# An adaLN block with sliding-window attention and a token-mixing MLP: normalization work moved between VectorE and GpSimd, the first MLP matmul split by token groups, another written order

## The chip, the cores and the metric

The kernel runs on one core of a Trainium2 chip. A core has five engines with a queue each: TensorE (PE) multiplies matrices from SBUF into PSUM, ScalarE (ACT) evaluates functions, VectorE (DVE) and GpSimd (POOL) do elementwise work, and SyncE (SP) issues DMA transfers. Each engine takes its instructions in order and waits on semaphores where an instruction needs another engine's result. [...]

The metric is the device time of one execution in microseconds. The time before is the median of three runs. A profile of one further execution gives the time of every instruction.

## The reference

One sequence of 2048 tokens with 512 features, in bf16. A condition vector `c` gives six modulation vectors; a windowed attention of 32 heads of 16 features and an MLP over the token axis follow.

```python
mod = (silu(c) @ w_mod).reshape(1, 6, 1, -1)
sa, ca, ga, sb, cb, gb = mod[:, 0], ..., mod[:, 5]
h = layernorm(x) * (1 + ca) + sa
x = x + ga * attention(h, wqkv, wo)      # 32 heads, key j for query i if 0 <= i - j < 256
h = layernorm(x) * (1 + cb) + sb
x = x + gb * B(h)
# B: h = layernorm(h); u = gelu(einsum('bsd,sf->bdf', h, w1) + b1)
#    y = einsum('bdf,fs->bds', u, w2) + b2; transposed back     w1: 2048 x 1792
```

So three layer norms are computed for each token: one ahead of the attention, one behind it with its modulation, and one inside the MLP. The MLP's first matmul sums over all 2048 tokens and gives 1792 rows of 512 features; the second sums over the 1792.

## The kernel before

**Token groups.** The tokens are worked on in four groups G of 512, each of four tiles of 128 tokens (16 tiles `x0` to `x15` in SBUF). For each group, `proj` normalizes and modulates the input, transposes it, and computes queries, keys and values; `attention` does the windowed attention; `post` does the output projection, the second layer norm with its modulation, and the MLP's layer norm. The result of a tile is `hb`, the MLP's input.

**Attention.** It goes by 75 chunks of 512 score columns for four heads at once (15 in group 0, 20 in each other). For chunk i, TensorE computes the scores (S) into four PSUM banks (`pss`, three, and `psb`, one), ScalarE takes the exponential in two instructions (EA of 128x1536 and EB of 128x512) into a bf16 tile `et`, and VectorE multiplies the columns at the window's edges by a 0/1 mask (M, 512 or 1024 columns in all). `et` has seven buffers. Two units of 256 queries share five chunks; when a unit's last mask is done, TensorE multiplies its tiles with the values and with ones (AV, into `po`), ScalarE takes logarithm and exponential of the sums (`lz`), and VectorE multiplies (OT). Keys are stored in two copies with alternate features set to zero (`KT`, split by GpSimd from `kb`), and values in block form (`VT`, placed by GpSimd from `vb` and `vs`).

**Shared banks.** Four banks are the scores' (five with `psb`'s two buffers). Three others, `od0` to `od2`, are shared by everything else that TensorE computes while attention runs: projections, AV, output projection, partial sums of the MLP. Such a bank is free again when its eviction, mostly on VectorE, is done.

**Layer norms.** `norm_ops` gives VectorE one statistics instruction per tile. For the groups of four tiles (`quiet`), GpSimd then combines the statistics in eight instructions on 4 or 8 columns: mean, variance, the power -0.5 (`rs`) and the product of mean and `rs` (`nm`). The first tiles and the last group use ScalarE instead. In `post`, groups 0 to 2 are normalized on GpSimd (`n2`, tile `xn2`, shown as `xn` in the profile), then modulated (`m2`: a product with `bc_cb1` and a sum with `bc_sb`, on VectorE but for two tiles on GpSimd), then normalized again on GpSimd (`hb`).

**The MLP's first matmul.** While attention still runs, `partials` computes for each of the 14 blocks fc of 128 rows the sum over the first 1024 tokens (eight matmuls `p`, evicted as `part`), from chunk 52 on. Its weights come in pieces of 512 KB (1024 tokens x 256 rows). The rest of the sum, over the last 1024 tokens, is `mlp1` (`u`): it starts when the last chunk's attention is under way, adds `part` on VectorE (`ga`), takes the GELU on ScalarE, and multiplies with `bc_gb`. The last part of the kernel is the second matmul (`py`), 16 tiles of 14 matmuls each, added to the input and stored.

**The opening.** SyncE issues the loads of the first two token tiles, two of the four parts of `w_mod`, then `wqkv` in pieces; ScalarE's queue issues the condition vector and the two other parts. TensorE runs filler matmuls (`warm`, eight pairs) on a zero tile; eight of them come first, the rest between and behind the transposes and the modulation matmuls (`fm`). The first key matmul stands behind all of them.

**What sets the order.** All this is a list of operations with names, engines and dependencies. A written list `ORDER` gives the sequence in which they are emitted, and so the order on every engine's queue; a table `CHOSEN` gives the engine where an operation may run on several. A function walks the list and emits. The constants for costs and ready times in the code (`X_READY` and others) take no part in the emitted program when the order is written out: they decide only which of the three shared banks an operation takes.

Almost every instruction of the profile has line 234, that of the wrapper that emits it, so groups are told apart by their tiles.

Of the kernel before, what the change touches and what calls it, by code (L numbers as in the profile page):

```python
# [13 lines left out]
P = 128  # L14
# [12 lines left out]
PART_A = 3  # L27
PART_AT = 20.0
# [3 lines left out]
X_READY = [3.0, 3.75, 11.7, 12.0]  # L32
MOD_READY = [4.7, 6.7, 6.9, 7.4]
W_READY = [8.35, 9.25, 9.25, 11.0, 14.0]
# [26 lines left out]
    2, 38, 3, 9, 40, 1, 10, 11, 4, 12, 41, 13, 14, 42, 16, 39, 8, 43, 44, 45, 17, 46, 18, 48, 47, 19, 6, 20, 7, 51,  # L61
    50, 49, 5, 52, 0, 53, 54, 56, 55, 57, 70, 58, 71, 126, 72, 75, 127, 73, 59, 76, 80, 60, 123, 81, 74, 128, 130,
    77, 61, 78, 82, 85, 131, 79, 86, 84, 83, 89, 63, 62, 132, 134, 87, 64, 124, 135, 65, 15, 67, 68, 66, 90, 88, 69,
    136, 138, 139, 264, 93, 121, 94, 129, 106, 91, 95, 142, 140, 96, 107, 265, 143, 98, 97, 92, 108, 266, 144, 166,
    111, 167, 267, 109, 99, 145, 268, 168, 100, 170, 112, 171, 110, 146, 133, 147, 113, 151, 137, 148, 174, 172,
    115, 152, 149, 173, 102, 175, 103, 150, 114, 141, 27, 104, 153, 269, 184, 176, 28, 494, 154, 156, 185, 271, 270,
    155, 157, 29, 116, 273, 177, 117, 272, 158, 188, 186, 118, 161, 159, 275, 120, 189, 495, 24, 119, 276, 187, 160,
    190, 198, 496, 101, 25, 199, 274, 724, 21, 22, 169, 162, 105, 200, 26, 202, 163, 23, 30, 203, 31, 497, 178, 191,
    498, 164, 206, 204, 179, 165, 32, 207, 180, 192, 193, 277, 194, 278, 181, 216, 208, 182, 279, 217, 183, 280,
    499, 36, 286, 281, 287, 218, 220, 282, 283, 195, 288, 221, 284, 209, 289, 292, 285, 222, 501, 725, 332, 196,  # L70
    293, 333, 290, 205, 298, 201, 299, 503, 294, 334, 336, 197, 295, 210, 291, 337, 37, 211, 34, 33, 212, 505, 125,
    500, 223, 314, 213, 340, 35, 338, 315, 300, 341, 956, 957, 219, 302, 310, 316, 311, 214, 335, 350, 296, 342,
    224, 312, 225, 351, 726, 226, 313, 301, 233, 215, 339, 352, 354, 504, 234, 727, 355, 297, 304, 235, 305, 728,
    356, 343, 364, 230, 227, 306, 365, 231, 357, 307, 317, 318, 232, 228, 368, 958, 366, 353, 344, 229, 369, 345,
    242, 122, 239, 319, 370, 308, 372, 236, 373, 371, 502, 237, 303, 243, 240, 374, 238, 506, 309, 382, 346, 383,
    241, 321, 320, 244, 322, 358, 384, 245, 386, 359, 347, 387, 323, 959, 246, 360, 375, 328, 348, 396, 388, 329,
    349, 508, 397, 324, 325, 330, 507, 361, 400, 729, 398, 367, 401, 516, 326, 247, 517, 399, 376, 518, 362, 404,
    402, 377, 389, 520, 519, 405, 513, 385, 363, 514, 731, 960, 248, 378, 406, 414, 249, 522, 515, 379, 415, 523,
    255, 327, 390, 391, 524, 380, 331, 732, 418, 416, 392, 381, 250, 419, 526, 509, 525, 510, 403, 521, 393, 407,
    428, 730, 420, 528, 511, 733, 429, 529, 408, 251, 734, 530, 430, 432, 417, 512, 540, 394, 256, 433, 531, 409,  # L80
# [32 lines left out]
]  # L113
CHOSEN = {
    "ACT": [
        48, 50, 72, 74, 95, 1017, 1034, 1039,
    ],
    "DVE": [
        47, 49, 51, 52, 66, 69, 77, 79, 82, 84, 87, 91, 97, 100, 104, 108, 110, 113, 115, 118, 120, 248, 250, 252, 254,
        277, 278, 281, 285, 288, 294, 300, 306, 312, 316, 319, 323, 326, 330, 478, 480, 482, 484, 507, 508, 511, 515,  # L120
        518, 524, 530, 536, 542, 546, 549, 553, 556, 560, 708, 710, 737, 738, 741, 745, 748, 754, 760, 764, 767, 771,
        774, 780, 786, 790, 968, 973, 979, 984, 990, 995, 1001, 1006, 1012, 1023, 1028,
    ],
    "POOL": [
        712, 714,
    ],
}
BATCH = True
# [1225 lines left out]
```

## Time and profile before

| | us |
|---|---|
| median of three runs | 257.79 (255.44 to 257.80) |
| profiled execution | 258.61 |
| its span, first to last instruction | 256.8 |
| first exponential starts | 12.89 |
| scores of the last chunk start | 172.40 |
| TensorE busy | 241.1 |
| VectorE busy | 200.6 |
| ScalarE busy | 179.9 |
| GpSimd busy | 133.0 |

The granted TensorE clock is 0.993 of full speed on average.

Lines of a timeline are: start, duration, engine, line, operation, output and inputs by the program's names, count. Lines with shapes ("128x512") give partitions and elements. Busy time of TensorE counts a matmul from start to modelled end, and matmuls overlap; a stretch in which it is 100% busy is not always one at its peak. Instructions on one engine can overlap at their ends too: a VectorE eviction of 0.68 us is followed by the next one 0.60 us after its start.

### The profile page before, as it was taken

The numbers are of one execution on the slowest core, as the hardware profiler recorded it, in microseconds if no ns is written. First come the engines' busy times: TensorE is split into PE (matmuls) and PEld (weight loads), VectorE is DVE, ScalarE is ACT, GpSimd is POOL, SyncE is SP. The second block draws the span as 40 slices with busy tenths as digits, with TensorE's granted clock in tenths as the row PEclk, the third lists the DMA queues.
The fourth block names the chain that finished last, engine by engine and source line by source line (L and its number), as shares of the span: only waits on it lengthen the run. The fifth ranks groups of instructions, "written<-read, shape, count | busy, mean of one in ns | idle before, by whom it ended". The sixth has DMA issues, their size and how long they took to land.

```text
span 256.8 us, 8133 instructions
## 1 busy us (share of the span) xinstructions
PE 241.1 (94%) x3427; PEld 122.2 (48%) x3427; DVE 200.6 (78%) x392; ACT 179.9 (70%) x255; POOL 133.0 (52%) x237
## 2 busy tenths in 40 slices
PE   7988989899998999979999999999999999999994
PEld 2665635444443454434545454446444444444443
DVE  4589999998899999998658879799869864444442
ACT  4399999999999999998999999998138510000000
POOL 8288977999999897896914389190000000000000
PEclk9999999999999999989999999999999999999999
DMA  7998360246254400060030003351899601111111
GB/s 222 326 349 252 12 80 3 42 114 159 61 120 60 116 3 3 9 182 0 5 92 14 3 3 84 106 142 37 326 332 387 232 22 41 58 48 41 41 43 41
DMA packets 41341, 27.02 MB, mean 105 GB/s; under 512 B 11992, under 2 KB 37208, under 8 KB 41304
## 3 DMA queue, kind: packets, MB, share of 16 engines
q1 hardware_dynamic: 41008, 25.97, 36.2%
q8 instruction: 27, 0.44, 0.7%
q10 hardware_dynamic: 296, 0.53, 0.6%
q14 instruction: 10, 0.08, 0.1%
HBM read 22.03 MB, written 2.10 MB: 94 GB/s over the span
## 4 chain that ended last, share of the span: by engine, by line
PE 61%; POOL 12%; DVE 10%; ACT 8%; issue 4%; DMA 3%; SPq 0%; DVEq 0%; POOLq 0%
PE pu L234 20%; PE py L234 19%; PE po L234 7%; ACT et L234 6%; PE pss L234 6%; POOL VT L234 4%; PE pa L234 3%; DVE et L234 3%; POOL xn L234 3%; POOL KT L234 2%; PE pk L234 2%; DMA w1p<-in_B_w_dram 2%; PE pv L234 2%; ACT lz L234 1%; DVE vb L234 1%
## 5 line engine op out<-in xcount | busy, mean ns | idle before, releaser
L234 ACT ACTIVATE et<-pss 128x1536 bf16<-128x1536 f32 x75 | 110.8, 1477 | 3.3 <-PE psb L234 1.7
L234 PE MATMUL pu<-hb,w1p 128*128 128x512 bf16 x224 | 52.6, 380 | 0.0
L234 DVE TENSOR_TENSOR et<-et,maskt 128x1024 bf16<-128x1024 bf16 (+2 forms) x79 | 48.5, 628 | 2.7 <-ACT et L234 2.6
L234 PE MATMUL py<-guT,w2r 128*128 128x512 bf16 (+1 forms) x238 | 48.7, 366 | 0.5 <-DVE otile L234 0.5
L234 ACT ACTIVATE et<-psb 128x512 bf16<-128x512 f32 x75 | 46.9, 626 | 0.0
L234 PE MATMUL pss<-QT,KT 32*128 32x64 bf16 (+3 forms) x720 | 30.0, 232 | 6.6 <-ACT et L234 5.0
L234 PEld LDWEIGHTS <-w2r 128*128 128x128 bf16 x238 | 23.3, 98 | 26.0 <-issue 0.7
L234 PE MATMUL po<-et,VT 128*32 128x64 bf16 (+3 forms) x960 | 32.3, 237 | 1.0 <-DVE kb L234 0.6
L234 PEld LDWEIGHTS <-w1p 128*128 128x128 bf16 x224 | 20.4, 98 | 25.0 <-issue 2.5
L234 PE MATMUL po<-et,ones_bd 128*32 128x256 bf16 (+3 forms) x624 | 32.0, 271 | 0.0
L234 POOL TENSOR_SCALAR KT<-kb,mask_par 128x512 bf16<-128x512 bf16 (+1 forms) x38 | 27.4, 732 | 7.2 <-ACT kb L234 5.8
L234 DVE TENSOR_TENSOR otile<-py,xr 128x512 bf16<-128x512 f32 (+1 forms) x17 | 11.2, 660 | 25.3 <-PE py L234 25.2
L234 PEld LDWEIGHTS <-KT 32*128 32x128 bf16 x960 | 15.8, 93 | 31.1 <-issue 28.9
L234 PE MATMUL psb<-QT,KT 32*128 32x64 bf16 (+3 forms) x240 | 29.5, 232 | 0.0
L234 PEld LDWEIGHTS <-VT 128*32 128x32 bf16 x960 | 19.6, 97 | 12.9 <-issue 10.7
L234 POOL TENSOR_SCALAR xn<-x,rs,nm 128x512 bf16<-128x512 bf16 x24 | 22.8, 951 | 1.4 <-DVE h L234 0.5
L234 DVE BATCH_NORM_STATS2 st<-x 128x6 f32<-128x512 bf16 x32 | 21.4, 682 | 2.2 <-DMA x<-in_A_x_dram 2.1
L234 PE MATMUL pk<-h1T,wqkv 128*128 128x256 bf16 (+2 forms) x108 | 21.3, 326 | 0.6 <-DVE vb L234 0.5
L234 PEld LDWEIGHTS <-wqkv 128*128 128x128 bf16 x164 | 13.8, 99 | 13.4 <-issue 6.0
L234 DVE TENSOR_TENSOR OT<-po,lz 128x256 bf16<-128x256 f32 x32 | 13.3, 416 | 8.2 <-ACT lz L234 8.2
L234 PE MATMUL pv<-wqkv,h1T 128*64 128x256 bf16 (+1 forms) x112 | 17.2, 321 | 0.4 <-DVE OT L234 0.4
L234 PE MATMUL pa<-wod,OT 128*128 128x512 bf16 x64 | 17.0, 380 | 0.4 <-DVE kb L234 0.2
(99 smaller groups left out, 324.1 us busy)
## 6 DMA issues: line engine op xcount, KB each, us to landing
w1p<-in_B_w_dram SPq DMA_DIRECT2D x14, 512.0 KB, 5.0
w2r<-in_B_w_dram SPq DMA_DIRECT2D x14, 512.0 KB, 7.8
x<-in_A_x_dram SPq DMA_DIRECT2D x16, 128.0 KB, 5.2
wmod<-in_w_mod_dram SPq DMA_DIRECT2D x4, 512.0 KB, 8.6
out_dram<-otile SPq DMA_DIRECT2D x15, 128.0 KB, 1.7
wqkv<-in_A_wqkv_dram SPq DMA_DIRECT2D x4, 256.0 KB, 4.9
vs<-vb SPq DMA_DIRECT2D x24, 32.0 KB, 3.0
wmod<-in_w_mod_dram ACTq DMA_DIRECT2D x2, 256.0 KB, 3.7
```

What stands on the lines that cost most here:

```text
L234: ins = call(*args, **kwargs)
```

## The change

1. **Second layer norm and modulation.** The normalization `n2` goes. Two scalar-tensor-tensor instructions on VectorE compute (x - mean) * `bc_cb1` and then that * `rs` + `bc_sb`, for all 16 tiles.
2. **Statistics.** Five of the small instructions that combine the statistics go to VectorE (a tensor-tensor and four scalar-tensor-tensor ones); GpSimd keeps the power and, for two of the three norms, the product `nm`.
3. **Masks.** M may run on VectorE or GpSimd; 21 of the 75 run on GpSimd by the new table (chunks 1, 7, 25, 31, 41 to 46, 50, 51, 59, 62 to 64, 66 to 69, 73), and two instructions of the third group's input modulation.
4. **First MLP matmul.** For blocks 0 to 9, the first 1024 tokens become two groups of 512: the first (`pE` below, four matmuls, evicted as `part`) needs only group 0's `hb`, the second is added to it on VectorE (`pd`). Blocks 10 to 13 stay whole. Weights come in quarters of 256 KB.
5. **Opening.** The second token tile is loaded by ScalarE's queue, ahead of the condition vector; the parts of `w_mod` change queues. The fillers are eight, then two, one and two matmuls at fixed places; two stand between the last `fm` and the first key matmul.
6. **Order.** `ORDER` and `CHOSEN` are written anew.

In the new order, the first groups of blocks 0 to 9 stand between the scores of chunks 42 and 56, and the second groups follow from chunk 58; the last group's projections reach to chunk 60 (58 before). Around one place, TensorE's two lists are:

```
before: ... S45 q3.1 AV40 S46 S47 AV41 AV42 k3.2 S48 AV42 AV43 AV44 S49 v3.2 k3.3 S50 ...
after:  ... S45 pE1 k3.0 S46 q3.0 AV40 q3.0 S47 AV41 AV42 v3.0 S48 v3.1 AV42 AV43 S49 ...
```

GpSimd's and VectorE's new lists around the masks of chunks 41 to 46 (l2pw is the power; "ke", "qe", "ve", "peE" are evictions):

```
GpSimd:  M42 l2pw M41 M43 M44 M45 M46 vo M50 kk M51 ...
VectorE: OT M40 peE2 m2 peE1 ke m2 OT qe m2 ve M47 ve OT m2 peE4 M48 M49 peE5 ...
```

The core of the diff:

```diff
     load_x(0)
-    load_x(1)
-    load_mod(0, nc.scalar)
-    load_mod(1, dma)
-    load_mod(2, nc.scalar)
-    load_mod(3, dma)
+    load_mod(0, dma)
+    load_mod(1, nc.scalar)
+    load_mod(2, dma)
+    load_mod(3, nc.scalar)
...
+    load_x(1, nc.scalar)
+    nc.scalar.dma_start(out=c4[:], in_=c.rearrange("o (j p) -> (o j) p", p=P))
...
+    warms = warm_ops(4, 2, [])
...
+    warms += warm_ops(2, 1, [o5])
...
+        fms[0].deps.append(transposed[0][0])
+        warms.extend(warm_ops(1, 1, fms[0:1]))
+        fms[1].deps.append(warms[-1])
+        warms.extend(warm_ops(2, 1, fms[-1:]))
...
-            po.tensor_tensor(out=mv[:], in0=st[:, :, 1:3], in1=st[:, :, 4:6], op=ALU.add)
-            po.tensor_tensor(out=mv[:], in0=mv[:], in1=halves[:, 0:n, :], op=ALU.mult)
-            po.tensor_tensor(out=sq[:], in0=st[:, :, 1], in1=st[:, :, 4], op=ALU.subtract)
-            po.tensor_tensor(out=sq[:], in0=sq[:], in1=sq[:], op=ALU.mult)
-            po.tensor_scalar(out=sq[:], in0=sq[:], scalar1=0.25, scalar2=EPS, op0=ALU.mult, op1=ALU.add)
-            po.tensor_tensor(out=sq[:], in0=sq[:], in1=mv[:, :, 1], op=ALU.add)
-            po.tensor_tensor(out=rs[:], in0=sq[:], in1=power[:, 0:n], op=ALU.pow)
-            po.tensor_tensor(out=nm[:], in0=mv[:, :, 0], in1=rs[:], op=ALU.mult)
+            var = mv[:, :, 1]
+            ve.tensor_tensor(out=sq[:], in0=st[:, :, 1], in1=st[:, :, 4], op=ALU.subtract)
+            ve.scalar_tensor_tensor(out=var, in0=st[:, :, 2], scalar=D * EPS, in1=st[:, :, 5], op0=ALU.add, op1=ALU.add)
+            ve.scalar_tensor_tensor(out=mv[:, :, 0], in0=sq[:], scalar=-0.5, in1=st[:, :, 4], op0=ALU.mult, op1=ALU.subtract)
+            ve.scalar_tensor_tensor(out=sq[:], in0=sq[:], scalar=0.25, in1=sq[:], op0=ALU.mult, op1=ALU.mult)
+            ve.scalar_tensor_tensor(out=var, in0=var, scalar=1.0 / D, in1=sq[:], op0=ALU.mult, op1=ALU.add)
+
+        def e_pw(e):
+            _, mv, rs, nm = box[key]
+            po.tensor_tensor(out=rs[:], in0=mv[:, :, 1], in1=power[:, 0:n], op=ALU.pow)
+            if tag != "l2":
+                po.tensor_tensor(out=nm[:], in0=mv[:, :, 0], in1=rs[:], op=ALU.mult)
...
-            def e_n(e, tl=tl, j=j):
-                xn2[tl] = late.tile([P, D], BF, name="xn2", tag="xn2")
-                normalize(e, xn2[tl][:], xres[4 * G + tl][:], ("l2", G, own[0]), j)
-
-            def e_m(e, tl=tl):
+            def e_m(e, tl=tl, j=j):
+                _, mv, rs, _ = box["l2", G, own[0]]
                 u = h2[tl] = late.tile([P, D], BF, name="h2", tag="h2", bufs=4)
-                ENGINE[e].tensor_tensor(out=u[:], in0=xn2[tl][:], in1=bc_cb1[:], op=ALU.mult)
-                ENGINE[e].tensor_tensor(out=u[:], in0=u[:], in1=bc_sb[:], op=ALU.add)
+                ve.scalar_tensor_tensor(
+                    out=u[:], in0=xres[4 * G + tl][:], scalar=mv[:, j, 0:1], in1=bc_cb1[:],
+                    op0=ALU.add if shifted else ALU.subtract, op1=ALU.mult,
+                )
+                ve.scalar_tensor_tensor(
+                    out=u[:], in0=u[:], scalar=rs[:, j : j + 1], in1=bc_sb[:], op0=ALU.mult, op1=ALU.add,
+                )
...
+        def group(fc, lo, deps, pos, first):
+            hi = 8 if first and fc >= EARLY or not first else 4
...
+            def e_pe(e):
+                if first:
+                    part[fc] = box["A" if fc < EARLY else "B"].tile([P, D], F32, name=f"part{fc}")
+                    copy(e, part[fc][:], box["p", fc][:])
+                else:
+                    ve.tensor_tensor(out=part[fc][:], in0=box["p", fc][:], in1=part[fc][:], op=ALU.add)
...
+        for fc in range(EARLY):
+            pos = start_of(2) + EARLY_AT + fc * EARLY_STEP
+            early[fc] = group(fc, 0, [loads[fc // 2, 0], *done[:4]], pos, True)
...
+            if fc < EARLY:
+                g = group(fc, 4, [loads[fc // 2, 1], *done[4:]], pos, False)
+            else:
+                g = group(fc, 0, [loads[fc // 2, 0], loads[fc // 2, 1], *done], pos, True)
...
-                    ve.tensor_tensor(out=dst, in0=dst, in1=msk, op=ALU.mult)
+                    ENGINE[e].tensor_tensor(out=dst, in0=dst, in1=msk, op=ALU.mult)
```

`normalize` is unchanged. In the new order the load of the last exchanged value tile (`vs`) stands on SyncE's queue behind ten loads of `w1` quarters.

## The prediction

> **What bounds the kernel now.** I read the busy shares first, then busy time by stages, then the timeline of each boundary. Over the whole span TensorE looks like the only limit:
>
> ```profile
> PE 241.1 (94%) x3427; PEld 122.2 (48%) x3427; DVE 200.6 (78%) x392; ACT 179.9 (70%) x255; POOL 133.0 (52%) x237
> ```
>
> The stages say otherwise (columns: stretch, its length, then busy us of PE, PEld, DVE, ACT, POOL; clock, DMA share, GB/s):
>
> ```profile
> 12.90:20.00 7.10, 5.94 (x95) 4.32 (x94) 6.37 (x16) 6.58 (x11) 6.05 (x11) 1.00 1.10 348
> 20.00:50.00 30.00, 26.94 (x570) 15.56 (x568) 29.10 (x62) 29.98 (x42) 25.56 (x45) 1.00 0.38 70
> 50.00:98.00 48.00, 44.67 (x850) 21.93 (x851) 45.93 (x89) 47.41 (x65) 44.55 (x76) 1.00 0.40 87
> 98.00:120.00 22.00, 19.29 (x375) 9.69 (x373) 20.55 (x38) 20.64 (x27) 17.35 (x32) 0.92 0.21 57
> 120.00:172.40 52.40, 52.22 (x915) 25.62 (x914) 41.71 (x74) 51.72 (x72) 31.29 (x49) 1.00 0.21 55
> ```
>
> From the first exponential (12.89) to the scores of the last chunk (172.40) ScalarE is busy 156.3 of 159.5 us: it waits 0.52 + 0.02 + 0.59 + 1.36 + 0.68 = 3.2 us in all. That stage is ScalarE's: 75 chunks at 1.477 + 0.626 us of exponentials, plus logarithms and reciprocals. From 172.40 to 251.6 TensorE never stops; its chain is fixed work (last attention outputs, the rest of the partial sums, 56 pairs of the second half, 238 output matmuls), and the end is at 256.8: **84.4 us of tail**. So the time is: first exponential + ScalarE's work + ScalarE's waits + tail. VectorE (95 to 97% from 20 to 98) and GpSimd (93%) count only where they make ScalarE or that tail wait.
>
> **Opening.** The first exponential is late by a queue, not by data:
>
> ```profile
> 7.98 2.72 PE L234 MATMUL pss<-warm 128*128 128x512 bf16 x6
> 8.50 0.86 DVE L234 TENSOR_SCALAR h1T<-h1T,modFM 128x256 bf16<-128x256 bf16 x3
> 10.49 0.49 PE L234 MATMUL pss<-h1T,wqkv 128*128 128x128 bf16 x4
> ```
>
> The operands are ready at 9.36, but six filler matmuls stand in front of the first key matmul. After the change two stand there, one more between the first two modulation matmuls, and 16 fillers become 13. Without the queue the key matmul comes 10.49 - 9.36 = 1.1 us earlier. The weights' landing (4.7 to 5.5 us after an issue at 2.7) isn't later, as SyncE issues three loads ahead of them, not four. Against it: all four modulation matmul groups now follow the second transpose, two of which ran before it. I take -1.0, bounds -1.3 (the second input tile, landing at 4.42 behind the first, comes by its own queue: 0.28 us of VectorE's wait) and 0.
>
> **ScalarE's work.** From the two written orders: behind the first exponential it loses two 128x256 evictions (0.38 each) and gains two such and one of 128x512 (0.59 long, 0.48 start to start, as for the partial sums): +0.5. The exponentials, logarithms and reciprocals are the same. This has no cover: the stage is ScalarE's.
>
> **VectorE and GpSimd, by durations.** VectorE loses 21 masks: 13 of 128x1024 (0.750), 7 of 128x512 (0.506), one of the first group (0.79): 14.1; 14 products and 14 sums of the modulation (0.435 + 0.580): 14.2; four normalizations (0.61): 2.4; two modulations of the transposed input (0.428): 0.9. It gains 32 scalar-tensor-tensor instructions; the nearest row is the one with an f32 output, 0.743: 23.8 (from below the tensor-tensor rows, 0.435 to 0.580: 13.9 to 18.6). Then nine groups of five instructions on 4 columns (0.15 to 0.18 each): 7.2; ten additions into partial sums (0.688): 6.9. Sum +6.3 us. GpSimd loses seven of eight small instructions per statistics group (six in the two kinds that keep the product): a group takes 3.7 to 3.9 now and 1.1 to 1.4 after, nine times 2.5: 22; twelve normalizations (0.951): 11.4; two modulations (1.310 + 1.594): 5.8. It gains the masks: not in the trace there; nearest are its tensor-tensor rows, 1.310 for 512 columns, so 2.6 for 1024: 13 x 2.6 + 7 x 1.3 + 2.0 = 45 (from below, by 0.76, its shortest 512-column form with one input, 26), and the two modulations, 0.9 each. Sum +8. Neither is on the path by its sum: VectorE's additions fall mostly behind 98, where it idles 1.5 + 10.7 us, and GpSimd's masks too (17 of the 21 belong to chunks 41 and later), where it idles 4.7 + 21.1. What hides them is ScalarE's stage; if VectorE falls behind, its evictions hold the three PSUM banks that projections, attention outputs and partial sums share, and scores queued behind them on TensorE make ScalarE wait.
>
> **First MLP matmul split.** The number of matmuls is the same. Ten half groups move ahead, between chunks 42 and 56; projections of the last group and the output projection of group 2 move behind them, so that TensorE's work ahead of chunk 55 is equal within 1 us, and behind the last scores the same pairs are left in both orders, less one attention output of 0.2 us. The tail therefore stays: **-0.2**. The split does fill one hole:
>
> ```profile
> 110.00:114.00 4.00, 2.09 (x62) 1.23 (x64) 3.93 (x8) 3.79 (x6) 4.00 (x5) 0.89 0.73 193
> 114.00:118.00 4.00, 4.00 (x92) 2.20 (x88) 3.97 (x9) 2.94 (x4) 2.24 (x7) 0.69 0.32 95
> ```
>
> TensorE idles 1.9 us, its granted clock falls to 0.69 for the next stretch, and ScalarE waits 1.06 us there for scores behind projections at that clock. Two scores stand next to each other in that place now; afterwards half groups stand between all of them. I take away 1.2 of the 1.36 us, and 0.3 of the 0.52 in the opening (normalized tiles late on VectorE). Bounds: nothing, and all 3.2 us but 0.5. Weight loads become 28 of 256 KB in place of 14 of 512 KB; the last exchange of value rows stands on SyncE's queue behind one of them that waits for the fourth completed partial sum (scores 63 to 64), and its reader is first needed behind score 71: eight chunks of 2.1 us cover it.
>
> **The port.** What a mask on GpSimd does to VectorE can be read where GpSimd does such work now:
>
> ```profile
> 153.94 1.20 POOL L234 TENSOR_TENSOR h<-xn,bc_cb 128x512 bf16<-128x512 bf16 x1
> 155.22 1.48 POOL L234 TENSOR_TENSOR h<-h,bc_sb 128x512 bf16<-128x512 bf16 x1
> ```
>
> ```profile
> 154.05 1.64 DVE L234 TENSOR_TENSOR et<-et,maskt 128x1024 bf16<-128x1024 bf16 x1
> 155.61 0.41 DVE L234 TENSOR_TENSOR OT<-po,lz 128x256 bf16<-128x256 f32 x1
> 155.94 1.04 DVE L234 TENSOR_TENSOR et<-et,maskt 128x512 bf16<-128x512 bf16 x1
> ```
>
> The mask at 154.05, usually 0.67, ends 0.55 us after GpSimd's product at 155.14; the one at 155.94 ends 0.27 after GpSimd's sum at 156.70; the product at 155.61, with an input in PSUM, isn't held. So two-input work from SBUF goes in turns. [...] Both new modulation instructions read two SBUF tensors. Bounds for ScalarE's waits by this: 0, as VectorE and GpSimd are full from 20 to 98 at no loss, and +6 (below). I take +1.0, nearer to the former row.
>
> **Sum**: -1.0 + 0.5 - 1.2 - 0.3 + 1.0 - 0.2 = -1.2 us. On the profiled execution, 258.61 (span 256.8 and 1.8 around it), that is 257.4; this execution lies 0.8 over the median of the runs, 257.79, so I give **256.6**, with 255.2 to 258.8 for this case by itself. Chance 0.34.
>
> **Rivals.**
> *ScalarE closes up*: its waits fall to 0.5 everywhere as GpSimd's statistics chains (3.8 us to 1.4) and normalizations stop delaying. -1.0 + 0.5 - 2.7 - 0.2 = -3.4: 254.4, at best 253.6. For it: 39 us less of other work on GpSimd, which is 93% busy to 98. Against it: only 0.6 us are lost there now. 0.32.
> *The port decides* (slower): chunks 41 to 46 go to GpSimd in a train, 62 to 69 in a second. In the first, four modulations meet it: the first instruction waits for the running mask (1.2 on average), GpSimd takes the port between the two, the second waits 1.3 to 2.6: some 3 us each, 9 for the three inside the train, against 2.6 us of slack: from chunk 41 to 49 (17 us) VectorE's list has 14.4 us (seven evictions of 0.68, four masks of 2.5 together, three outputs of 0.416, four modulations of 1.49). Its lateness grows from 0 to 6.4 us; the banks that scores stand behind come free in the first half of that, some 2.5 us late; twice that with the second train. -1.0 + 0.5 - 1.5 + 5.0 - 0.2 = +2.8: 260.6, and up to 262 with the +6. It makes the kernel slower once ScalarE's waits sum to over 3.9 us, and by over 1% from 6.5; here they are 6.7. For it the rows above; against it the outputs' seven buffers, some 10 us of room for a mask. 0.24.
> *The opening stays*: the condition vector is now issued behind a 128 KB tile on ScalarE's queue; if it lands 1 us later than 2.3, the chain of silu stands ahead of the second statistics on VectorE and the 1.0 is lost: -0.2, 257.6. 0.10.
>
> Faster by over 1% (under 255.2; 1% is about what a measurement here can tell from no change): the second case, and a little of the first, 0.34. Within 1%: the rest of the first and the last, 0.42. Slower: the port, 0.24. The range reaches from the best of the second case to the port's upper bound, 253.4 to 262.0.
>
> **What would show it.** First key matmul at 9.4 to 9.7; first exponential at 11.7 to 12.1; last scores at 171 to 172 and 84.2 us behind them; no low clock at 110 to 118; ScalarE's waits about 2.7 us. The port would show as VectorE's masks and modulations of over 1.5 us, in chunks 41 to 46, with ScalarE waiting. Wrong I'd be if the tail changed its length, or if partial sums added on VectorE delayed the second half of the MLP.

## The result and the profile after

The change makes the kernel slower: a median of 276.54 us (274.2 to 278.99) beside 257.04 us for the kernel before, a ratio of 1.074 with a 95% interval of 1.064 to 1.084. One of these four runs (278.99), one of e8 and one of e11 below were in a slower state, and the ratios and the medians from here on leave them out, so that the changed kernel stands at 276.21. The forecast was 256.6 us, no change, with a range up to 262.0.

The profiled execution of the changed kernel took 274.2 us, span 272.5, which is 15.7 us more than the span before. First the busy shares of its page:

```profile
PE 241.2 (89%) x3424; PEld 121.7 (45%) x3424; DVE 223.7 (82%) x422; ACT 181.5 (67%) x256; POOL 145.4 (53%) x186
```

TensorE has the same work (241.2 us for 241.1) in a longer span. VectorE grew by 23.1 us, where the sum of durations in the prediction gave 6.3; this busy time includes time for which an instruction is held (2.55 us in a row below, for an estimated 0.743). Next the busy time by stages, with the first exponential (14.13) and the scores of the last chunk (187.29) as ends; columns as in the table of before: stretch, length, busy us of PE, PEld, DVE, ACT and POOL, granted clock, DMA share, GB/s.

```profile
14.13:20.00 5.87, 5.27 (x88) 4.03 (x90) 5.68 (x16) 5.84 (x9) 5.31 (x9) 1.00 1.10 349
20.00:50.00 30.00, 25.22 (x496) 14.60 (x490) 29.51 (x67) 28.02 (x40) 23.80 (x32) 1.00 0.36 70
50.00:98.00 48.00, 41.54 (x843) 20.85 (x842) 45.71 (x86) 45.98 (x63) 39.70 (x53) 1.00 0.33 63
98.00:120.00 22.00, 18.14 (x322) 8.66 (x323) 21.34 (x37) 20.61 (x27) 18.46 (x20) 1.00 0.01 2
120.00:187.29 67.29, 59.45 (x1080) 29.35 (x1074) 62.04 (x104) 58.19 (x77) 45.47 (x47) 1.00 0.30 82
```

The 15.7 us lie in three places: the first exponential is 1.24 us later (14.13 for 12.89), the stretch up to the last scores takes 173.16 us in place of 159.51 (+13.65), and the tail is 85.2 us for 84.4 (+0.8). In the middle stretch ScalarE now idles 173.16 - 158.63 = 14.5 us, before 3.2. So the loss is ScalarE waiting, above all behind 120 (9.1 us), and there VectorE is busy 92% of the time, where it was 80% before. What it waits for is in the table of ScalarE's waits (us in total, times, longest):

```profile
ACT et L239 <- PE psb L239: 9.5, 12, 2.3
ACT lz L239 <- PE po L239: 3.3, 3, 2.0
ACT et L239 <- PE pss L239: 2.1, 3, 1.1
```

All of these rows name TensorE, because it is the engine that wrote last. Why TensorE is late is seen in the timeline of the first train of masks on GpSimd (start, duration, engine, line, operation; in brackets the idle time before and what ended it):

```profile
114.33 10.31 POOL L239 TENSOR_TENSOR et<-et,maskt 128x1024 bf16<-128x1024 bf16 x5
...
114.46 2.55 DVE L239 SCALAR_TENSOR_TENSOR h<-x,mv,bc_cb 128x512 bf16<-128x512 bf16 x1
...
117.12 1.45 DVE L239 SCALAR_TENSOR_TENSOR h<-h,rs,bc_sb 128x512 bf16<-128x512 bf16 x1
...
118.49 0.68 DVE L239 COPY part<-pu 128x512 f32<-128x512 f32 x1
...
119.22 0.59 PE L239 MATMUL pq<-h1T,wqkv 128*128 128x512 bf16 x2 [2.46 <-DVE part L239]
...
121.36 1.45 ACT L239 ACTIVATE et<-pss 128x1536 bf16<-128x1536 f32 x1 [2.32 <-PE psb L239]
```

This is one chain from left to right. Two modulation instructions take 2.55 and 1.45 us beside the five masks on GpSimd, the eviction of a half group (`part`) behind them on VectorE's queue is late, the query projection waits 2.46 us for that bank, the scores behind the projection on TensorE's queue are late, and ScalarE waits 2.32 us. Two more waits follow the same train, 0.94 us at 124.51 and 1.10 at 127.86: 4.4 us for one train, where the rival "the port decides" had 2.5 ("the port" is its name for the turns of the rows at 154 us in the kernel before; what the two engines share there is not shown by a run). In the second train, from 163.75 on, the modulation instructions take 2.08, 1.45, 1.41 and 2.49 us, and ScalarE waits 2.02 us for an attention output whose bank comes free behind them. It also waits 1.20 us at 171.41, but there TensorE had first waited 1.13 us for a piece of `w1`, so that this wait isn't the hold alone. The masks themselves are not waited for: in the table of waits none of TensorE or ScalarE is put down to a mask on GpSimd. The averages of the same instructions over the whole kernel (busy us, mean ns of one):

```profile
L239 POOL TENSOR_TENSOR et<-et,maskt 128x1024 bf16<-128x1024 bf16 x13 | 29.1, 2244 | 8.5 <-ACT et L239 8.2
L239 DVE SCALAR_TENSOR_TENSOR h<-x,mv,bc_cb 128x512 bf16<-128x512 bf16 x16 | 21.9, 1366 | 0.0
L239 DVE SCALAR_TENSOR_TENSOR h<-h,rs,bc_sb 128x512 bf16<-128x512 bf16 x16 | 17.8, 1113 | 0.9
```

The two instructions of the modulation, estimated at 0.743 us each, take 1.37 and 1.11.

The opening is late in a way of its own. TensorE's rows in the changed kernel:

```profile
7.96 0.54 PE L239 MATMUL ps_fm<-sT,wmod 128*128 128x1 bf16 x16
9.51 0.37 PE L239 MATMUL ps_fm<-sT,wmod 128*128 128x1 bf16 x8 [1.01 <-DMA wmod<-in_w_mod_dram]
9.74 1.01 PE L239 MATMUL pss<-warm 128*128 128x512 bf16 x2
11.01 0.58 PE L239 MATMUL pss<-h1T,wqkv 128*128 128x128 bf16 x4 [0.25 <-DVE h1T L239]
```

The last group of modulation matmuls waits 1.01 us for the last part of `w_mod`, and the stages behind it show the granted clock (the third figure from the right) falling to a half:

```profile
8.00:10.00 2.00, 0.99 (x26) 0.76 (x25) 0.25 (x3) 0.23 (x1) 0.00 (x0) 0.84 1.14 312
10.00:12.00 2.00, 1.75 (x11) 0.99 (x10) 1.38 (x7) 0.60 (x1) 0.00 (x0) 0.50 1.10 338
```

The first key matmul starts at 11.01, not at 9.4 to 9.7.

### The profile page after: what moved, and what is told of

Read it like the earlier page. It is cut to its first block, busy times and chain, and to the rows that moved or that the text cites. A ratio compares the mean times of both kernels' runs of the same rounds, so it can differ in the third digit from the quotient of the medians.

```text
span 272.5 us, 8135 instructions
## 1 busy us (share of the span) xinstructions
PE 241.2 (89%) x3424; PEld 121.7 (45%) x3424; DVE 223.7 (82%) x422; ACT 181.5 (67%) x256; POOL 145.4 (53%) x186
## 4 chain that ended last, share of the span: by engine, by line
PE 41%; DVE 38%; ACT 11%; issue 6%; DMA 3%; DVEq 0%; ACTq 0%
PE py L239 18%; DVE h L239 11%; PE pu L239 10%; ACT et L239 8%; DVE et L239 5%; DVE st L239 5%; PE po L239 3%; PE pss L239 2%; DVE OT L239 2%; DVE part L239 2%; DMA wmod<-in_w_mod_dram 2%; ACT lz L239 2%; PE pk L239 2%; DVE h1T L239 2%; DVE x L239 2%
## 5 line engine op out<-in xcount | busy, mean ns | idle before, releaser
L239 ACT ACTIVATE et<-pss 128x1536 bf16<-128x1536 f32 x75 | 109.5, 1460 | 12.2 <-PE psb L239 9.5
L239 POOL TENSOR_TENSOR et<-et,maskt 128x1024 bf16<-128x1024 bf16 (+2 forms) x22 | 41.0, 1877 | 13.2 <-ACT et L239 13.0
L239 ACT ACTIVATE et<-psb 128x512 bf16<-128x512 f32 x75 | 45.6, 608 | 0.0
L239 PE MATMUL pu<-hb,w1s 128*128 128x512 bf16 x152 | 39.2, 380 | 1.8 <-DMA w1s<-in_B_w_dram 1.1
L239 DVE TENSOR_TENSOR et<-et,maskt 128x1024 bf16<-128x1024 bf16 (+2 forms) x57 | 34.8, 625 | 0.8 <-ACT et L239 0.7
L239 POOL TENSOR_SCALAR KT<-kb,mask_par 128x512 bf16<-128x512 bf16 (+1 forms) x38 | 26.5, 708 | 12.7 <-issue 6.4
L239 PE MATMUL po<-et,ones_bd 128*32 128x256 bf16 (+3 forms) x624 | 31.3, 268 | 0.0
L239 PEld LDWEIGHTS <-wqkv 128*128 128x128 bf16 x164 | 14.5, 101 | 18.5 <-issue 10.6
L239 PEld LDWEIGHTS <-w1s 128*128 128x128 bf16 x152 | 13.5, 97 | 18.8 <-issue 4.6
L239 DVE SCALAR_TENSOR_TENSOR h<-x,mv,bc_cb 128x512 bf16<-128x512 bf16 x16 | 21.9, 1366 | 0.0
L239 DVE SCALAR_TENSOR_TENSOR h<-h,rs,bc_sb 128x512 bf16<-128x512 bf16 x16 | 17.8, 1113 | 0.9
```

The lines of the kernel that those rows point to most:

```text
L239: ins = call(*args, **kwargs)
```

## The experiments

Runs e1 to e4 ask which of the parts costs the most, e5 to e8 separate the opening, the order and the two moves of normalization work, e9 to e12 test what those suggested. Ratios are to the kernel before, which had a median of 256.1 to 256.3 us in these runs; e5 to e8 ran on a second chip.

| run | median us | ratio (95%) |
|---|---|---|
| e1 changed, all masks on VectorE | 269.07 | 1.049 (1.043 to 1.055) |
| e2 changed, GpSimd writes in place of its masks | 263.97 | 1.030 (1.025 to 1.035) |
| e3 changed, second norm and modulation as before | 279.00 | 1.090 (1.084 to 1.095) |
| e4 before, the 21 masks on GpSimd | 279.27 | 1.089 (1.083 to 1.094) |
| e5 changed, old opening loads | 272.89 | 1.063 (1.057 to 1.070) |
| e6 changed, masks, modulation, statistics as before | 266.91 | 1.039 (1.033 to 1.045) |
| e7 before, fused modulation | 261.99 | 1.020 (1.014 to 1.027) |
| e8 before, statistics on VectorE | 258.71 | 1.008 (1.005 to 1.012) |
| e9 before, two fillers in place of six | 256.43 | 1.002 (0.999 to 1.005) |
| e10 as e5, two zero fills moved | 271.55 | 1.059 (1.054 to 1.064) |
| e11 as e10, all masks on VectorE | 263.75 | 1.033 (1.025 to 1.040) |
| e12 before, fused modulation and statistics on VectorE | 264.12 | 1.028 (1.022 to 1.034) |

### The masks (e1, e2, e4)

e1 undoes the masks alone:

```diff
-                    ENGINE[e].tensor_tensor(out=dst, in0=dst, in1=msk, op=ALU.mult)
+                    ve.tensor_tensor(out=dst, in0=dst, in1=msk, op=ALU.mult)
```

> The changed kernel with all masks on VectorE again; nothing else differs. Port theory (two-input VectorE work and GpSimd's masks take turns at SBUF, so the masks' 2 us blocks hold the new modulation instructions): although VectorE gets about 14 us of work back, the scalar-tensor-tensor means fall from 1.37 and 1.11 towards 0.8 to 1.0, and the time falls by 8 to 14 us, to 262 to 268. Overload theory (VectorE has too much work whatever GpSimd does): 280 or more. Order theory (the new order and the split of the first MLP matmul are the loss): 276 within 3.

It gives 7.1 us back (276.2 to 269.1), a little less than the port theory said, and the modulation instructions come down to 0.81 us:

```profile
L239 DVE SCALAR_TENSOR_TENSOR h<-h,rs,bc_sb 128x512 bf16<-128x512 bf16 x16 | 13.0, 814 | 1.0
L239 DVE SCALAR_TENSOR_TENSOR h<-x,mv,bc_cb 128x512 bf16<-128x512 bf16 x16 | 13.0, 813 | 0.0
```

ScalarE's waits for scores in this profile are 6.7 us, in the changed kernel's 12.2. So taking 21 masks off VectorE cost time, although VectorE loses 14 us of its own work by it. e2 asks what it is in those masks that holds VectorE: their length on GpSimd's queue, or their reading of SBUF. GpSimd does two fills with ones over the same columns, which take 1.57 us for 1024 columns where they stand in a train (ten fills in 7.87 us below), against 2.06 for a mask (five in 10.31).

```diff
-                    ENGINE[e].tensor_tensor(out=dst, in0=dst, in1=msk, op=ALU.mult)
+                    if e == "DVE":
+                        ve.tensor_tensor(out=dst, in0=dst, in1=msk, op=ALU.mult)
+                    else:
+                        for _ in range(2):
+                            po.memset(dst, 1.0)
```

> The changed kernel, where each mask on GpSimd is replaced by two writes of ones to the same columns: GpSimd stays as busy at the same places (about 1.9 us for 1024 columns), waits for the same data and is waited for in the same way, but reads nothing from SBUF. The masking of those 21 chunks is left out. Port theory, if reading SBUF is what holds VectorE: scalar-tensor-tensor near 0.8 to 1.0, time 258 to 266. If any use of SBUF by GpSimd holds it: 274 to 278. Theory that GpSimd's masks are late for the attention outputs: 274 to 278. Overload and order theories: 274 to 278.

263.97 us, and in the same place of the timeline nothing is held:

```profile
113.64 7.87 POOL L239 MEMSET et<- 128x1024 bf16 x10
...
113.92 0.74 DVE L239 SCALAR_TENSOR_TENSOR h<-x,mv,bc_cb 128x512 bf16<-128x512 bf16 x1
114.78 0.75 DVE L239 SCALAR_TENSOR_TENSOR h<-h,rs,bc_sb 128x512 bf16<-128x512 bf16 x1
...
115.45 0.68 DVE L239 COPY part<-pu 128x512 f32<-128x512 f32 x1
```

With ten fills running on GpSimd, the two-input instructions take 0.74 and 0.75 us, the evictions behind them are on time, and ScalarE's waits for scores are 3.9 us. So in the same place the first of these instructions took 0.74 us beside GpSimd's fills, which only write, and 2.55 beside its masks, which also read; the second took 0.75 and 1.45.

e2 is also shorter work for GpSimd than the masks (1.57 for 2.06), so it does not say that the whole 12.2 us between it and the changed kernel is the hold. e4 puts the masks of the same 21 chunks (`ON_GPSIMD`) on GpSimd in the kernel before:

```diff
-                    ve.tensor_tensor(out=dst, in0=dst, in1=msk, op=ALU.mult)
+                    (po if i in ON_GPSIMD else ve).tensor_tensor(out=dst, in0=dst, in1=msk, op=ALU.mult)
```

> The kernel before with the same 21 masks on GpSimd and nothing else changed. Port theory: 5 to 10 us slower, 262 to 267, with VectorE's tensor-tensor instructions held up to 2 us. Overload theory: VectorE loses 14 us of work, so 254 to 257. Order theory: 256 to 258.

That costs 23 us, far more than any of the theories said and three times what the masks cost in the changed kernel, and it is another mechanism. The stages of e4:

```profile
98.00:120.00 22.00, 18.08 (x325) 8.90 (x329) 17.19 (x30) 19.52 (x27) 19.82 (x29) 0.98 0.11 29
120.00:140.00 20.00, 13.61 (x234) 6.73 (x232) 11.97 (x20) 11.64 (x15) 18.70 (x26) 0.68 0.11 32
```

From 120 to 140 GpSimd is busy 18.7 of 20 us while VectorE is busy 12.0 and ScalarE 11.6: GpSimd itself has become the bound. It still carries twelve more normalizations and the whole statistics chains there. The masks wait in its queue, attention outputs wait for the masks (10.7 us in five waits over the kernel, where the changed kernel has none), and TensorE's granted clock falls to 0.68. In the changed kernel, whose other parts relieve GpSimd, the masks cost a third of this, and they still don't pay.

### Second norm and modulation, statistics (e3, e7, e8, e12)

e3 takes the fused modulation out of the changed kernel, e7 puts it alone into the kernel before. The edit of e7, which e3 has the other way round:

```diff
-                normalize(e, xn2[tl][:], xres[4 * G + tl][:], ("l2", G, own[0]), j)
...
-                ENGINE[e].tensor_tensor(out=u[:], in0=xn2[tl][:], in1=bc_cb1[:], op=ALU.mult)
-                ENGINE[e].tensor_tensor(out=u[:], in0=u[:], in1=bc_sb[:], op=ALU.add)
+                ve.scalar_tensor_tensor(out=u[:], in0=xres[4 * G + tl][:], scalar=mv[:, j, 0:1], in1=bc_cb1[:],
+                    op0=ALU.add if shifted else ALU.subtract, op1=ALU.mult)
+                ve.scalar_tensor_tensor(out=u[:], in0=u[:], scalar=rs[:, j : j + 1], in1=bc_sb[:], op0=ALU.mult, op1=ALU.add)
```

> The changed kernel with the old second layer norm: a normalization on GpSimd (VectorE in the last group), then product and sum as tensor-tensor on VectorE. Port theory: the instructions that are held get shorter and GpSimd gets 12 normalizations more; the masks still hold VectorE; 268 to 273. Overload theory: VectorE loses about 8 us of work of its own and 16 of holding: 262 to 268. Order theory: 276 within 3.

> The kernel before with the fused normalization and modulation on VectorE in its places of the old order; masks, statistics, split and opening as before. Theory 'the fusion is a gain': twelve normalizations of 0.95 us and two modulations leave GpSimd, VectorE gets some 8 us more; as taking it out of the changed kernel cost 2.5 us, it gives 0 to 2 us here: 254.5 to 257. Rival 'VectorE is full': it is 95 to 97% busy from 20 to 98 us, and the added work there (some 5 us in three groups) comes straight through evictions to the scores: 259 to 263, with ScalarE's waits 3 to 6 us up.

The two answers have opposite signs. In the changed kernel the fusion is a gain, where the port and the overload theories expected a loss: without it 279.0 us, 2.8 more, with ratio intervals that only just meet (1.084 to 1.095 and 1.064 to 1.084). There GpSimd has the masks, and with the normalizations back on it VectorE waits for it:

```profile
L239 DVE TENSOR_TENSOR h<-xn,bc_cb 128x512 bf16<-128x512 bf16 x16 | 12.8, 798 | 11.5 <-POOL xn L239 11.0
```

In the kernel before, the fusion is a loss of 5.9 us (261.99 for 256.1), which is what the rival "VectorE is full" expected. ScalarE's waits for scores go up to 6.3 us for the fourth bank alone, 1.7 before:

```profile
ACT et L234 <- PE psb L234: 6.3, 8, 2.6
```

The longest of them, 2.63 us up to 118.59, is the hole that the prediction had seen at 110 to 118, where ScalarE lost 1.06 us before: the fusion widens it.

e8 puts the five small instructions on VectorE into the kernel before:

```diff
-            po.tensor_tensor(out=mv[:], in0=st[:, :, 1:3], in1=st[:, :, 4:6], op=ALU.add)
...
+            ve.tensor_tensor(out=sq[:], in0=st[:, :, 1], in1=st[:, :, 4], op=ALU.subtract)
+            ve.scalar_tensor_tensor(out=var, in0=st[:, :, 2], scalar=D * EPS, in1=st[:, :, 5], op0=ALU.add, op1=ALU.add)
...
```

> The kernel before with the five small instructions of each statistics group on VectorE; everything else as before. Theory 'shorter chain': GpSimd's chain of 3.7 us becomes 1.1 to 1.4, VectorE gets nine times 0.7 to 1.1 us: 0 to 1 us gained, 255 to 257. Rival 'VectorE is full': 6 to 10 us more of VectorE, most of it where it is 95 to 97% busy: 258 to 262.

258.71 us: 2.6 more, a ratio of 1.008 (1.005 to 1.012). The shorter chain on GpSimd gains nothing that shows; the work added to VectorE, 7.2 us by the estimate of the prediction, shows in part. e12 has both parts together in the old order:

> The kernel before with both the fused modulation and the statistics on VectorE, in the old order without the split. If the two costs add: 256.1 + 5.9 + 2.7 = 264.7, between 263.5 and 266. If this is the same time as the repaired changed kernel's, the split of the first matmul and the new order cost nothing by themselves; if this is 3 us or more above it, they gain. Rival 'GpSimd's shorter chain helps the fusion': 261 to 263.

264.12 us, in the range that the sum of the two losses gives. The stages of e12 say where:

```profile
50.00:98.00 48.00, 41.53 (x829) 20.57 (x828) 46.90 (x97) 44.74 (x61) 35.53 (x52) 1.00 0.40 88
98.00:120.00 22.00, 18.14 (x328) 8.74 (x327) 21.42 (x40) 21.49 (x29) 13.53 (x17) 1.00 0.20 56
120.00:140.00 20.00, 19.12 (x352) 9.68 (x355) 14.63 (x31) 17.05 (x26) 9.85 (x14) 0.91 0.11 32
```

VectorE is busy 97 to 98% from 50 to 120, GpSimd idles 12.5 us in 50 to 98 (3.5 before), and ScalarE now idles 3.3 us in 50 to 98 (0.6 before). Up to the last scores it idles 9.0 us (3.2 before). Another 2.95 us of that stand in 120 to 140, at a clock of 0.91, with 2.62 in one wait at 122.63. It comes from the same queue: up to 120.26 a key projection waits 1.72 us for the product OT, which stands behind a modulation on VectorE's queue. These two parts of the change move work from an engine with slack to the one without.

### The opening (e5, e9)

e5 puts the old loads into the changed kernel and keeps the new fillers:

```diff
-    load_x(1, nc.scalar)
-    nc.scalar.dma_start(out=c4[:], in_=c.rearrange("o (j p) -> (o j) p", p=P))
-    load_mod(0, dma)
-    load_mod(1, nc.scalar)
...
+    nc.scalar.dma_start(out=c4[:], in_=c.rearrange("o (j p) -> (o j) p", p=P))
+    load_x(1)
+    load_mod(0, nc.scalar)
+    load_mod(1, dma)
...
```

> The changed kernel with the opening's loads as they were: the second token tile on SyncE's queue, the condition vector first on ScalarE's queue, the four parts of w_mod on their old queues. The fillers and everything else stay changed. Theory 'a late weight load': in the changed kernel the last part of w_mod holds the last modulation matmuls until 9.51 us, and TensorE's granted clock falls to 0.50 behind that wait. With the old loads that part is there by about 7.5, the clock stays near 1.0, the first key matmul starts at 9.2 to 9.8 (11.01 in the changed kernel) and the first exponential at 11.7 to 12.4 (14.1); the time is 1.5 to 2.5 us under the changed kernel's 276.5: 274 to 275. Rival 'too few fillers': the clock falls in any case, the first exponential stays at 13.5 to 14, the time at 276 to 277.

272.89 us, 3.3 less by the medians, more than either theory said. The intervals of the two ratios overlap (1.057 to 1.070 and 1.064 to 1.084), so the time alone does not settle it. The opening of its profile is 3 us earlier than the changed kernel's:

```profile
6.95 0.74 PE L239 MATMUL ps_fm<-sT,wmod 128*128 128x1 bf16 x24
7.76 0.38 PE L239 MATMUL pss<-warm 128*128 128x512 bf16 x1
8.81 0.38 PE L239 MATMUL pss<-h1T,wqkv 128*128 128x128 bf16 x4 [0.67 <-DVE h1T L239]
```

All modulation matmuls run through at 6.95, the clock stays at 1.00, the first key matmul starts at 8.81 and the first exponential at 11.10. The profiled span keeps only 1.0 of these 3.0 us (271.5 for 272.5), as later waits are longer: 3.34 us in place of 2.32 in the first train of masks. An opening varies between executions, so here are all eight profiles with the new fillers (TensorE's busy time is that of the 2 us from 6 to 8; the clock is that from 10 to 12):

| profile | loads | wait for `w_mod`, us | TensorE busy, us | clock | first exponential |
|---|---|---|---|---|---|
| changed | new | 1.01 | 1.20 | 0.50 | 14.13 |
| e1 | new | 1.50 | 1.11 | 0.50 | 15.84 |
| e2 | new | 1.94 | 0.96 | 0.50 | 16.04 |
| e3 | new | 0.73 | 1.31 | 0.50 | 14.23 |
| e6 | new | 0.61 | 1.11 | 0.50 | 14.76 |
| e5 | old | none | 1.92 | 1.00 | 11.10 |
| e10 | old | none | 1.98 | 1.00 | 11.15 |
| e11 | old | none | 1.37 | 0.50 | 13.40 |

The late part of `w_mod` and the late exponential come with the new loads in all five. But e11 has the low clock with the old loads, without that wait, so the rival "too few fillers" is not ruled out as a part of the loss. In the changed kernel the last part of `w_mod` is issued from ScalarE's queue at 3.4 us, behind a token tile, the condition vector and another part, while SyncE issues its four `wqkv` loads from 2.19 us on.

e9 tests the filler queue, on which the prediction's term of -1.0 stood, in the kernel before:

```diff
-                  lambda e, i=i: e_warm(e, 2, i == 0)
+                  lambda e, i=i: e_warm(e, {4: 0, 5: 1, 6: 1}.get(i, 2), i == 0)
```

> The kernel before with two filler matmuls in place of six ahead of the first key matmul; its loads and all else unchanged. Theory 'the queue of fillers': in executions where a filler takes 0.43 us from start to start the first key matmul stands 1.7 us earlier, up to the arrival of its operands: the first key matmul at 8.7 to 9.4 and the first exponential at 10.8 to 11.8 (12.89 in the profile of before; 11.3 and 10.7 in two later runs with the same opening, where a filler took 0.22); the time falls by 0.5 to 1.5 us: 254.6 to 255.6. Rival 'fillers keep the clock': with four fewer TensorE's granted clock falls to 0.5 to 0.8 behind 8 us, the first exponential comes at 13 to 14, and the time is 257 to 258.

256.43 us, a ratio of 1.002 (0.999 to 1.005): no gain. Its own profile shows the early opening (key matmul at 8.36, waiting 0.60 us for its operands; exponential at 10.74), but so did e4 and e7, which have the six fillers. In e4 these took 0.22 us from start to start:

```profile
7.95 1.24 PE L234 MATMUL pss<-warm 128*128 128x512 bf16 x5
9.03 0.39 PE L234 MATMUL pss<-h1T,wqkv 128*128 128x128 bf16 x4
```

In the profile before, six of them took 2.72 us, 0.42 from start to start. The late opening of the profile that the prediction read was a feature of that execution: openings with unchanged code gave a first exponential at 12.89, 12.7 and 12.9 (before, e8, e12) and at 11.3 and 10.7 (e4, e7). With only two fillers e9's granted clock stayed at 1.00, so its rival did not come true either.

### Order and split (e6, e10, e11)

e6 has masks, modulation and statistics as before, so that order, split and opening are left (edits: those of e1 and of e7 and e8 the other way round).

> The changed kernel with masks on VectorE alone, the normalization and modulation of the second norm as before, and the statistics as before: what is left of the change is the new order, the split of the first MLP matmul and the opening. Theory 'the split costs little': beside the opening (first exponential at 14 to 16 in place of 12.9) ScalarE waits 3 to 6 us from there to the last scores, tail 83 to 85: 259 to 263. Rival 'order and split are a loss of their own' (ten additions into partial sums of 0.69 us on VectorE, projections moved behind them, and an order that counts on GpSimd's masks): ScalarE waits 8 us or more, and the time is 265 to 270, as far from the kernel before as the run with masks alone on VectorE (269).

266.91 us, in the range of the rival. But it is no clean measure of order and split: the new order has normalizations in places where only the fused form is quick. At 80.13 VectorE waits 2.35 us for GpSimd's normalization, and ScalarE waits 2.17 us at 84.09 behind it. Taking parts back under an order written for others costs something of its own.

e10 tests one detail that all kernels with the new order had until then: a wait of ScalarE of 1.2 us between 38 and 44. In the changed kernel:

```profile
39.08 2.68 DVE L239 TENSOR_SCALAR h1T<-h1T,modFM 128x512 bf16<-128x512 bf16 x2
39.46 1.84 POOL L239 MEMSET VT<- 128x1024 bf16 x2
...
41.68 0.41 DVE L239 CAST QT<-pk 128x256 bf16<-128x256 f32 x1
```

The modulation of the transposed input, 0.40 us elsewhere, takes 2.37 us (395/398/2365 ns for least, median and most of the four). It ends at 41.76, 0.46 us behind GpSimd's two fills with zeros, which is about the time it takes alone, and the query eviction stands behind it. e10 has the loads of e5 and moves the two fills (125 and 123 in `ORDER`) behind two placements of values (302 and 303):

```diff
-    125,
...
-    123,
...
     302,
+    125,
...
     303,
+    123,
```

> The changed kernel with the old opening loads, and two of GpSimd's fills of the third value tile with zeros (128x1024 each) put behind two later placements of values in the order. Theory 'a fill holds VectorE's modulation of the transposed input': that instruction takes 2.37 us beside the two fills (0.40 elsewhere), the query eviction behind it is late, and ScalarE waits 1.2 us between 38 and 44 us. With the fills moved it takes 0.40, that wait is under 0.4, and the time is 0.5 to 1.2 us under the same kernel with the fills in place (272.9): 271.7 to 272.4. Rival: the instruction waits for its own input or the query matmul is late; it still takes over 2 us, and the time stays at 272.9.

271.55 us, 1.3 less than e5, with ratio intervals that overlap (1.054 to 1.064 and 1.057 to 1.070). The wait of ScalarE behind the query eviction, 1.26 us in e5, is gone, and so is the long instruction (least, median, most):

```profile
L186 DVE TENSOR_SCALAR h1T<-h1T,modFM x4: 396/401/586, 36.9 to 38.3; 128x512 bf16<-128x512 bf16 x4
```

Here GpSimd instructions that only write do hold VectorE, in a one-input `tensor_scalar` from bf16 to bf16 in SBUF: 2.37 us beside the two fills in the changed kernel, 0.59 at most with them moved. The two-input instructions beside the fills of e2 took 0.74 to 0.75. Why the one is held and the others are not is not shown.

e11 is e10 with the masks on VectorE:

> The changed kernel with three repairs: all masks on VectorE, the old opening loads, and the two fills moved. What is left is the fused modulation, the statistics on VectorE, the split and the order. If the losses add up: 276.5 - 7.5 - 3.65 - 1.0 = 264.4, between 263.5 and 265.5. Theory 'the rest is VectorE': ScalarE's waits of 5 to 8 us are left, all behind evictions on VectorE. Rival 'the three losses cover each other': 266 to 268.

263.75 us (263.53 to 267.35, the last being the profiled run, with the late opening of the table above), with 1.033 (1.025 to 1.040) beside 1.028 (1.022 to 1.034) for e12. The two differ by the order with its choice of engines for evictions, the split of the first matmul and the fillers, and their intervals overlap: these cost nothing that could be told here, and gain nothing. Now there is a chain of kernels from the one before to the changed one, each pair differing by the part named:

| from | to | part | us |
|---|---|---|---|
| before 256.2 | e12 264.1 | fused modulation and statistics on VectorE | +7.9 |
| e12 264.1 | e11 263.8 | order, split, new fillers | -0.4, not told from 0 |
| e11 263.8 | e10 271.6 | 21 masks on GpSimd | +7.8 |
| e10 271.6 | e5 272.9 | two zero fills beside VectorE's modulation | +1.3, intervals overlap |
| e5 272.9 | changed 276.2 | loads of the opening | +3.3, intervals overlap |

The first and third steps are clear of the noise; of the last two it is the traces that show a cost, and its size is uncertain. Nor do the parts add whatever the path. Under the new order the fused modulation and the statistics cost 2.2 us (e1 269.07, e6 266.91, intervals that only just overlap), not 7.9; and what e6 leaves of the change costs 10.8 us, of which the loads and the fills account for 4.6 by the table. So the +7.9 is a price in the old order, and that order and split cost nothing is shown only beside the fused modulation.

No version was faster than the kernel before: e9 is equal to it.

## Why the prediction was wrong

**The bound was right, its reading was not.** First exponential + ScalarE's work + its waits + tail accounts for the loss. The step that failed first is "Neither is on the path by its sum: VectorE's additions fall mostly behind 98 ... What hides them is ScalarE's stage". The durations were sized well: in e2, where nothing is held by masks, the 32 fused instructions take 24.5 us (23.8 estimated) and VectorE is 8.1 us busier than before (6.3). The step set this work at nothing, because 14.1 us of masks were to leave VectorE and because it idles behind 98. Measured, the fusion and the statistics cost +7.9 us in the old order (e12). Between 50 and 120 VectorE had 2.1 + 1.5 us of idle time, the fused instructions of the first groups fall there, and each adds 0.74 + 0.75 in place of 0.435 + 0.580; the work saved lay on GpSimd, where ScalarE was not waiting. In the sum over the whole kernel, work that leaves in one stage paid for work that comes in another.

**The turns of GpSimd and VectorE: right in kind, wrong in size, and not likely enough.** "I take +1.0, nearer to the former row" failed: the masks cost 7.1 (e1) to 7.8 us (e11 to e10). The rival's chain came out link by link: the first two modulation instructions are held 1.8 and 0.7 us over their 0.74 (it had 1.2, and 1.3 to 2.6), a bank is late by 2.46 us (2.5), and ScalarE waits 4.4 us behind the first train (2.5). The argument for the low value was that VectorE and GpSimd were already full "from 20 to 98 at no loss"; but there GpSimd ran normalizations, key splits and value copies of 0.5 to 0.95 us, and VectorE's masks still averaged 0.75 us. Five masks of 2.06 us in a row are another load.

**The opening: wrong sign.** "I take -1.0, bounds -1.3 ... and 0" stood on one profile and on the filler queue. The queue is worth nothing in the median (e9: 256.43 for 256.19), and with the new loads the first exponential came at 14.1 to 16.0 in five profiles (3.3 us by the medians of e5 and the changed kernel, with overlapping intervals). The step "The weights' landing ... isn't later, as SyncE issues three loads ahead of them" counted the projection weights and not the last part of `w_mod`, which the first key matmul needs just as much. The rival "the opening stays" had the condition vector late, which came true (`em` waited 1.7 us for it), but not the part of `w_mod` (a wait of 1.01 us) or the clock behind it (0.50).

**ScalarE's waits: wrong.** -1.5 was predicted for the holes, -0.5 with the +1.0 for the turns, and +11.3 came in all. The split did what the step said of the clock: no low clock at 110 to 118 (1.00, before 0.89 and 0.69). TensorE idles all the same, 4.2 us between 114 and 126, now waiting for banks.

**ScalarE's work: sized too low.** +0.5 was predicted; its busy time in the stretch rose by 158.63 - 156.3 = 2.3. The evictions in it sum to nearly the same in both. The rest may be that instructions behind a wait no longer overlap the end of the one before; that is argued, not shown.

**The tail: right within a microsecond.** -0.2 predicted, +0.8 measured (85.2). In e2 and e6, which have the same additions into partial sums, it was 84.0 and 84.5, so these do not delay the second half by anything that shows; in e1 it was 86.3, with a wait of 1.1 us for a piece of `w1`.

A part that no step had is the two zero fills, a wait of 1.2 us in the trace.

## What to carry to other kernels

Count moved work per engine and per stage, and only against the idle time of the engine that receives it in that stage; a saving on an engine that nobody waits for pays for nothing. Before an elementwise instruction goes to GpSimd, look at what VectorE's queue holds during it. Here a modulation that reads two SBUF tensors took 2.55 us beside masks (0.74 beside fills), a one-input bf16 `tensor_scalar` 2.37 beside two fills (0.40 elsewhere), and the eviction behind the modulation passed the delay on, to TensorE (a wait of 2.46 us) and to ScalarE (2.32). An opening should be read from several profiles, and with the last load that its first product needs.

## What the runs showed of the hardware

- Fills on GpSimd held one kind of VectorE instruction and not another: a one-input 128x512 bf16 `tensor_scalar` took 2.37 us in place of 0.40 beside two of them (changed kernel), and two-input instructions stayed at 0.74 to 0.75 us beside ten (e2).
- A scalar-tensor-tensor instruction on 128x512 took 0.74 to 0.75 us with a bf16 output (medians of e12) just as with an f32 one (0.743, mean of the kernel before); the tensor-tensor instructions that it replaced, with bf16 on all sides, took 0.435 and 0.580 (means of the kernel before).
- GpSimd's mask of 128x1024 took 2.06 us in a train (five in 10.31), 2.24 on the average (changed kernel), where VectorE took 0.74 (e1).
- Filler matmuls took 0.42 us (before) or 0.22 (e4) from start to start in the same place of the same opening, with a granted clock of 1.00 in both profiles. In e12 six fillers took the longer time at a granted clock of 0.50 (8 to 10 us). Why an execution has the one or the other was not settled.
- In six openings with the new fillers the granted clock was 0.50 from 10 to 12 us, in two it stayed at 1.00. The longest wait of TensorE between the last modulation matmuls and the first key matmul does not separate them: it was 0.67 us in e11, with the low clock, and 0.67 in e5 and e10, without it. In these eight the low clock goes with a TensorE that was less busy from 6 to 8 us: 0.96 to 1.37 of 2 us in the six, 1.92 and 1.98 in the two.
